# Multiplying decays out over 128 tokens in place of 64, with four working PSUM banks and an earlier VectorE step, in a fused gated-recurrence and ELU-layer kernel

## Chip, cores, metric

One core of one Trainium2 chip. The metric is device microseconds of one execution. Engine names: PE is TensorE, PEld its weight loads, DVE VectorE, ACT ScalarE, POOL GpSimd.

## The reference

```python
batch, n_heads, seq, head_dim = (4, 8, 768, 48)
for t in range(S):                       # complex state S, real output
    ar, ai = (a_re_n[:, :, t, :, None], a_im_n[:, :, t, :, None])
    new_re = ar * S_re - ai * S_im
    new_im = ar * S_im + ai * S_re
    kv = np.einsum('bhd,bhe->bhde', k[:, :, t], v[:, :, t])
    S_re, S_im = (new_re + kv, new_im)
    y[:, :, t] = np.einsum('bhd,bhde->bhe', q[:, :, t], S_re)
# then, on x = y as (3072, 384), with d_ff = 2048:
h = x @ w_in
g = np.where(h > 0.0, h, alpha * (np.exp(np.minimum(h, 0.0)) - 1.0))
return (g @ w_out).astype(np.float32)
```

The decay `a` is first cut to a magnitude of at most 0.999. The kernel works with its logarithm `l` (the magnitude) and its angle: sums over the tokens of a chunk, then exponentials and sines, turn the recurrence into matrix products inside a chunk plus a state carried between chunks.

## The kernel before

A unit is one tile of 128 tokens for two batches; there are 12 units (`u`). All matmuls are fp32. A program in slots interleaves the recurrence of one unit with the layer of earlier ones. Lines with "cut", and "..." within a call, mark what is left out.

```python
L = 64
def work(shape):                                   # working PSUM banks
    return ps.tile(shape, FP32, tag="w", bufs=3, name="w")
# ... cut ...
def ratios(u):                                     # GpSimd from the third unit on
    products(u).tensor_tensor(out=w, in0=x["ar"], in1=t, op=ALU.mult)
    products(u).tensor_tensor(out=t, in0=x["ai"], in1=t, op=ALU.mult)

def slopes(u):
    nc.vector.scalar_tensor_tensor(out=flat(t), in0=flat(w), ...)   # the angle's slope
    nc.vector.scalar_tensor_tensor(out=flat(lm), in0=flat(lm), ...) # l; needs no product of GpSimd
# ... cut ...
def scores(u, n):                                  # two 64-token blocks per head
    for h in range(H):
        for c in range(C // L):
            nc.tensor.matmul(t[ts(c, L), h], lhsT=x["kt", n][:, h, ts(c, L)],
                             rhs=x["qt", n][:, h, ts(c, L)], start=True, stop=True)
    nc.vector.tensor_tensor(out=x["a", n], in0=t, in1=mask..., op=ALU.mult)

def states(u, n):                                  # two states per tile
    for h in range(H):
        for c, g in enumerate(gs):
            nc.tensor.matmul(g[:, h], lhsT=x["kg"][ts(c, L), n, h],
                             rhs=vn[u % 2][ts(c, L), n, h, 0:D], start=True, stop=True)
    for c, g in enumerate(gs):                     # old None: first state, one product
        nc.vector.tensor_tensor(out=new_s, in0=g, in1=old, op=ALU.add)
        nc.gpsimd.tensor_tensor(out=new_s, in0=new_s, in1=wide, op=ALU.mult)

def values(u, n):                                  # output halves j, chunks c
    y = ps.tile([C, C // L, 512], FP32, tag="y", bufs=1, name="y")
    # a x v over 64 tokens for every (p, c, j), then state x q for every (p, c, j)
# ... cut ...
decays_of(u, r + 11, r + 12, r + 13.5, r + 14.5, r + 14.6, r + 15.5, r + 15.5, r + 15)
```

Of the kernel before, what the change touches and what calls it, by code (L numbers as in the profile page):

```python
# [10 lines left out]
FP32 = mybir.dt.float32  # L11
U32 = mybir.dt.uint32
AF = mybir.ActivationFunctionType
ALU = mybir.AluOpType
PSUM = bass.MemoryType.PSUM

C = 128
L = 64
CAP = 0.999
EPS = 1e-6  # L20
LEAST_RE = 0.7
# [46 lines left out]
HP = 64  # L68
# [436 lines left out]
def kernel(  # L505
# [12 lines left out]
    nc = tc.nc  # L518
    B, H, S, D = q.shape
    DM, DF = moe_w_in.shape[0], moe_w_out.shape[0]  # L520
    NI, NF = DM // C, DF // C
    NP = H // 2
    HD = H * D
    NB = 2
# [11 lines left out]
    ps = ctx.enter_context(tc.tile_pool(name="ps", bufs=1, space=PSUM))  # L536
    dram = ctx.enter_context(tc.tile_pool(name="dram", bufs=1, space=bass.MemoryType.DRAM))

    def const(a, name):
        a = np.ascontiguousarray(a, dtype=np.float32)  # L540
        t = cst.tile(list(a.shape), FP32, name=name)
        nc.sync.dma_start(out=t, in_=nc.inline_tensor(a, name=name + "_c").ap())
        return t
# [5 lines left out]

    i = np.arange(C)  # L550
    upto = i[:, None] <= i[None, :]
    own = i[:, None] // L == i[None, :] // L

    vn = [cst.tile([C, NB, H, HP], FP32, name=f"vn{n}") for n in range(2)]
    NR = 2 * NI * NF // (NI * WF)
# [3 lines left out]
    quarter = value(float(np.pi / 2), "quarter")  # L559

    def work(shape):
        return ps.tile(shape, FP32, tag="w", bufs=3, name="w")


    nat = [{} for _ in range(NU)]
# [97 lines left out]
    def flat(t):  # L663
        return t.rearrange("p n h d -> p (n h d)")
# [5 lines left out]
    def new(tag, bufs=1, shape=None):  # L670
        return sb.tile(shape or [C, NB, H, D], FP32, tag=tag, bufs=bufs, name=tag)
# [21 lines left out]
    def ratios(u):  # L693
# [2 lines left out]
        products(u).tensor_tensor(out=w, in0=x["ar"], in1=t, op=ALU.mult)  # L696
        products(u).tensor_tensor(out=t, in0=x["ai"], in1=t, op=ALU.mult)  # L697

    def slopes(u):
        x = nat[u]  # L700
        lm, e, w, t = x["m2"], x["e"], x["w"], x["t"]
        nc.vector.scalar_tensor_tensor(
            out=flat(t), in0=flat(w), scalar=-2.0, in1=flat(t), op0=ALU.add, op1=ALU.mult
        )
        nc.vector.scalar_tensor_tensor(  # L705
            out=flat(lm), in0=flat(lm), scalar=2 * float(np.log(CAP)), in1=flat(e),
            op0=ALU.min, op1=ALU.subtract,
        )
        x["l"] = lm

    def noted(u):

# [47 lines left out]
    def decays(u):  # L760
        x = nat[u]
        x["E"], x["F"] = new("n", 6), new("n", 6)
        x["T"] = new("T", 2, [2 * D, NB, C // L, H])
        for n in range(NB):
            t = work([C, HD])
            nc.tensor.matmul(  # L766
                t, lhsT=sum_logs, rhs=x["l"][:, n].rearrange("p h d -> p (h d)"),
                start=True, stop=True,
            )
            for key, sign in (("E", 1.0), ("F", -1.0)):  # L770
                nc.scalar.activation(  # L771
                    out=x[key][:, n].rearrange("p h d -> p (h d)"), in_=t, func=AF.Exp,
                    scale=sign,
                )
        ends = dram.tile([NB, C // L, H, D], FP32, tag="ends", bufs=2, name="ends")
        nc.scalar.dma_start(
            out=ends.rearrange("n c h d -> c n (h d)"),
            in_=x["E"][L - 1 :: L].rearrange("p n h d -> p n (h d)"),
        )
        x["ends"] = ends  # L780

# [9 lines left out]
    def gated(u):  # L791
        x = nat[u]
        shape = [C, NB * H, 2, D]
        for key, by in (("k", "F"), ("q", "E")):
            eng = products(u) if key == "k" else nc.vector
            g = x[key]
            eng.tensor_tensor(out=g, in0=g, in1=x[by], op=ALU.mult)
            o = new(key + "g", 1, shape)
            eng.tensor_tensor(  # L799
                out=o, in0=g.rearrange("p n h d -> p (n h) d").unsqueeze(2).to_broadcast(shape),  # L800
                in1=x["cs"], op=ALU.mult,
            )
            x[key + "g"] = o.rearrange("p (n h) i d -> p n h (i d)", n=NB)
        for i in range(2):
            nc.gpsimd.dma_start(
                out=x["T"][ts(i, D)].rearrange("p n c h -> p (n c h)"),
                in_=x["ends"].rearrange("n c h d -> d (n c h)"),
            )


# [10 lines left out]

    def scores(u, n):
        x = nat[u]
        t = work([C, H, L])
        for h in range(H):
            for c in range(C // L):
                nc.tensor.matmul(  # L827
                    t[ts(c, L), h], lhsT=x["kt", n][:, h, ts(c, L)],
                    rhs=x["qt", n][:, h, ts(c, L)], start=True, stop=True,
                )  # L830
        x["a", n] = new("a", 2, [C, H, L])
        nc.vector.tensor_tensor(  # L832
            out=x["a", n], in0=t, in1=mask.unsqueeze(1).to_broadcast([C, H, L]), op=ALU.mult
        )

    def states(u, n):

        x = nat[u]
        b, s = where(u)
        x["S", n] = [state.get(b + n)]  # L840
        if s == S - C:
            last = C // L - 1
        else:
            last = C // L
        gs = [work([2 * D, H, D]) for c in range(last)]
        for h in range(H):
            for c, g in enumerate(gs):
                nc.tensor.matmul(  # L848
                    g[:, h], lhsT=x["kg"][ts(c, L), n, h], rhs=vn[u % 2][ts(c, L), n, h, 0:D],
                    start=True, stop=True,  # L850
                )
        for c, g in enumerate(gs):
            old = x["S", n][-1]
            new_s = new("S", 9, [2 * D, H, D])
            wide = x["T"][:, n, c].unsqueeze(2).to_broadcast([2 * D, H, D])
            if old is None:
                nc.vector.tensor_tensor(out=new_s, in0=g, in1=wide, op=ALU.mult)
            else:
                nc.vector.tensor_tensor(out=new_s, in0=g, in1=old, op=ALU.add)  # L859
                nc.gpsimd.tensor_tensor(out=new_s, in0=new_s, in1=wide, op=ALU.mult)  # L860
            x["S", n].append(new_s)
        state[b + n] = x["S", n][-1]

    def values(u, n):
        x = nat[u]
        y = ps.tile([C, C // L, 512], FP32, tag="y", bufs=1, name="y")
        each = [(p, c, j) for p in range(NP) for c in range(C // L) for j in range(2)]
        for p, c, j in each:

            nc.tensor.matmul(  # L870
                y[ts(j, HP), c, ts(p, L)], lhsT=vn[u % 2][ts(c, L), n, 2 * p + j],
                rhs=x["a", n][ts(c, L), 2 * p + j], start=(p == 0), stop=False,
                skip_group_check=True,
            )
        for p, c, j in each:
            if x["S", n][c] is not None:
                nc.tensor.matmul(  # L877
                    y[ds(j * HP, D), c, ts(p, L)], lhsT=x["S", n][c][:, 2 * p + j],
                    rhs=x["qt", n][:, 2 * p + j, ts(c, L)], start=False, stop=False,
                    skip_group_check=True,  # L880
                )
        if n == 0:
            x["x"], x["y"] = new("x", 2, [C, NI, GT]), new("y", 1, [C, GT])

        nc.scalar.copy(  # L885
            out=x["x"][:, :, ts(n, C)].rearrange("p x (c t) -> p c x t", c=C // L),
            in_=y[:, :, 0 : NI * L].rearrange("p c (x t) -> p c x t", x=NI),
        )
        nc.scalar.copy(  # L889
            out=x["y"][:, ts(n, C)].rearrange("p (c t) -> p c t", c=C // L),  # L890
            in_=y[:, :, NI * L : NP * L],
        )

    def seam(u):
# [64 lines left out]
    load_a(0)  # L959
    ident = const(np.eye(C), "ident")  # L960
    sum_turns = const(upto / (2 * np.pi), "sum_turns")
    sum_logs = const((upto & own) * 0.5, "sum_logs")
    mask = const(upto[:, 0:L] | (i[:, None] >= L) & (i[:, None] - L <= i[None, 0:L]), "mask")
    for t in vn:
        nc.gpsimd.memset(t[:, :, :, D:HP], 0.0)
    ctx.enter_context(tc.manual_schedule())
# [29 lines left out]
        plan.append((at, len(plan), lambda: fn(*args)))  # L996

    def decays_of(u, *at):
        fns = squares, logarithms, ratios, slopes, noted, angles, carried, decays
        for x, fn in zip(at, fns):  # L1000
            put(x, fn, u)

# [23 lines left out]
    for at, fn, u in (  # L1026
        (-44, load_qk, 0), (-44, load_v, 0), (-42, load_a, 1), (-32.8, load_qk, 1), (-23.5, load_v, 1),
    ):
        put(at, fn, u)
    decays_of(0, -40, -39, -39, -38, -37.9, -38, -38, -35)  # L1030
    gates_of(0, -36.5, -36, -33)
    put(-34, warm, 30)
    values_of(0, -32, -31, -30, -29, -26, -28, -27, -25, -24, -23, -22)
    decays_of(1, -33.5, -32.5, -31.5, -30.8, -8, -30.7, -30.6, -26.5)
    gates_of(1, -27.5, -27, -22.5)
    values_of(1, -20, -19, -18, -17, -14, -16, -15, -13, -12, -11, -10)
    layer_of(0, 4, 20)
# [8 lines left out]
    for u in range(2, NU):  # L1046
        r = (u - 2) * SLOTS
        put(r, load_a, u)
        put(r + 1, load_v, u)
        put(r + 6, load_qk, u)  # L1050
        decays_of(u, r + 11, r + 12, r + 13.5, r + 14.5, r + 14.6, r + 15.5, r + 15.5, r + 15)
        gates_of(u, r + 17, r + 17.5, r + 19)
        values_of(u, *(r + 22 + x for x in (0, 1, 2, 3, 5, 4, 5, 6, 7, 8, 9)))
        layer_of(u, r + 36, r + 44)
# [42 lines left out]
```

## Time and profile before

| | before |
|---|---|
| median time | 790.8 us |
| TensorE busy, granted clock | 91%, 0.963 |
| period of a unit in the steady part | 58.70 us |
| TensorE's wait before the sum of logs | 19.2 us in 9 waits |

"Busy" adds up spans that overlap, so 91% is not time at the peak. The steady part is better read by its period, the distance between the starts of one unit's sum of logs and the next one's: whatever shortens the period is multiplied by the units.

```profile
493.85 0.96 DVE L702 SCALAR_TENSOR_TENSOR n<-n 128x768 f32<-128x768 f32 x1 [4.60 <-POOL n L697]
494.72 0.95 DVE L705 SCALAR_TENSOR_TENSOR n<-n 128x768 f32<-128x768 f32 x1
```

`l` (L705) stands behind the slope (L702), which needs GpSimd's two products (L696, L697), although `l` itself doesn't.

### The profile page before, as it was taken

What the parts mean: (1) busy time and instruction counts of PE and PEld (TensorE: products, weight loads), DVE (VectorE), ACT (ScalarE), POOL (GpSimd) and SP (SyncE); (2) the same over time, 40 slices, a digit from 0 to 9 for tenths busy, and PEclk for the clock granted to TensorE, in tenths of its full rate; (3) what the DMA queues carried; (4) which work ended last, traced back from release to release, by engine and by line L of the source; (5) the groups of instructions that cost most, each with busy time, mean ns of one, the idle gap of its engine ahead of it and who ended that gap; (6) DMA issues with size and microseconds to landing.
All of it is one profiled execution on the core that took longest, in us unless ns stands there. A gap on an engine that the chain in (4) does not pass through costs nothing.

```text
span 787.3 us, 12936 instructions
## 1 busy us (share of the span) xinstructions
PE 713.4 (91%) x5406; PEld 530.9 (67%) x5406; DVE 303.4 (39%) x394; ACT 388.4 (49%) x590; POOL 221.5 (28%) x206
## 2 busy tenths in 40 slices
PE   1566877999999999999999999999999999999996
PEld 0445766666587587587587587587587587686773
DVE  4659997521422531531531531531531531430110
ACT  6364237535456456456456456456456456552230
POOL 0023302122522523523523523523523513501000
PEclk9955799899999999999999999999999999999998
DMA  9997162320340540540540540530530630200000
GB/s 169 177 170 178 33 162 80 62 51 12 77 91 1 117 91 2 123 86 2 125 81 2 128 80 2 132 76 1 136 72 2 140 67 1 66 2 4 23 0 25
DMA packets 141452, 56.08 MB, mean 71 GB/s; under 512 B 128792, under 2 KB 133448, under 8 KB 140616
## 3 DMA queue, kind: packets, MB, share of 16 engines
q1 hardware_dynamic: 137536, 53.72, 31.6%
q0 software_dynamic: 3776, 1.36, 1.9%
q8 instruction: 44, 0.72, 0.4%
q14 instruction: 24, 0.20, 0.1%
q10 hardware_dynamic: 72, 0.07, 0.0%
HBM read 49.14 MB, written 4.79 MB: 68 GB/s over the span
## 4 chain that ended last, share of the span: by engine, by line
PE 75%; DVE 8%; POOL 5%; ACT 4%; issue 4%; DMA 2%; SPq 1%; POOLq 0%; DVEq 0%; ACTq 0%
PE mlp L911 29%; PE mlp L927 26%; PE w L819 6%; PE w L848 5%; PE w L827 3%; PE w L766 2%; POOL n L697 2%; POOL n L696 2%; PE w L744 2%; PE y L877 2%; DVE n L705 1%; DMA w<-in_moe_w_in_dram 1%; PE y L870 1%; POOL S L860 1%; DVE wf L42 1%
## 5 line engine op out<-in xcount | busy, mean ns | idle before, releaser
L911 PE MATMUL mlp<-x,w_in 128*128 128x256 f32 x1152 | 265.6, 386 | 4.0 <-DVE g L918 4.0
L927 PE MATMUL mlp<-w_out,g 128*128 128x384 f32 x768 | 261.9, 491 | 0.0
L911 PEld LDWEIGHTS mlp<-x,w_in 128*128 128x128 f32 x1152 | 218.9, 193 | 37.4 <-DVE g L918 4.4
L927 PEld LDWEIGHTS mlp<-w_out,g 128*128 128x128 f32 x768 | 142.2, 190 | 91.3
L918 DVE SCALAR_TENSOR_TENSOR g<-ee,mlp 128x512 f32<-128x512 f32 x96 | 66.0, 687 | 216.4 <-ACT ee L917 176.5
L916 ACT ACTIVATE ee<-mlp 128x512 f32<-128x512 f32 x96 | 57.2, 596 | 147.5 <-PE mlp L911 141.7
L860 POOL TENSOR_TENSOR S<-S,T 96x384 f32<-96x384 f32 x40 | 35.5, 888 | 251.4 <-DVE S L859 251.4
L917 ACT ACTIVATE ee<-ee 128x512 f32<-128x512 f32 x96 | 60.5, 630 | 2.8
L799 POOL TENSOR_TENSOR kg<-k,cs 128x1536 f32<-128x1536 f32 x10 | 48.1, 4814 | 16.8 <-issue 16.1
L680 POOL TENSOR_TENSOR n<-n 128x768 f32<-128x768 f32 x11 | 19.9, 1813 | 114.3 <-ACT n L678 114.3
L848 PEld LDWEIGHTS w<-vn,kg 64*96 64x96 f32 x704 | 37.3, 172 | 12.6 <-issue 9.0
L885 ACT COPY x<-y 128x384 f32<-128x384 f32 x24 | 11.5, 480 | 67.8 <-PE y L877 67.6
L848 PE MATMUL w<-vn,kg 64*96 64x48 f32 x704 | 40.5, 258 | 3.0 <-ACT n L771 3.0
L859 DVE TENSOR_TENSOR S<-w,S 96x384 f32<-96x384 f32 x40 | 22.1, 552 | 54.6 <-PE w L848 39.2
L933 ACT COPY o<-mlp 128x384 f32<-128x384 f32 x24 | 11.5, 480 | 61.7 <-PE mlp L927 59.7
L766 PE MATMUL w<-n,sum_logs 128*128 128x384 f32 x48 | 21.3, 568 | 20.7 <-DVE n L705 19.2
L832 DVE TENSOR_TENSOR a<-w,mask 128x512 f32<-128x512 f32 x24 | 16.5, 688 | 59.2 <-PE w L827 59.2
L820 ACT COPY qt<-w 96x512 f32<-96x512 f32 x48 | 25.5, 575 | 27.8 <-PE w L819 27.7
L899 POOL DMA_DIRECT2D x<-y x72 | 35.7, 503 | 4.5 <-ACT y L889 4.5
L758 POOL DMA_DIRECT2D carry<-n x10 | 5.1, 512 | 111.4 <-DVE n L752 93.0
L819 PE MATMUL w<-ident,qg 128*96 128x128 f32 x192 | 27.2, 286 | 9.7 <-DVE qg L799 9.0
L819 PE MATMUL w<-ident,kg 128*96 128x128 f32 x192 | 26.9, 284 | 9.7 <-ACT qt L820 9.6
(74 smaller groups left out, 756.0 us busy)
## 6 DMA issues: line engine op xcount, KB each, us to landing
w<-in_moe_w_out_dram SPq DMA_DIRECT2D x16, 768.0 KB
w<-in_moe_w_in_dram SPq DMA_DIRECT2D x8, 768.0 KB
ar<-in_a_re_dram SPq DMA_DIRECT2D x24, 192.0 KB
ai<-in_a_im_dram SPq DMA_DIRECT2D x24, 192.0 KB
w<-in_moe_w_in_dram SPq DMA_DIRECT2D x12, 384.0 KB
q<-in_q_dram SPq DMA_DIRECT2D x24, 192.0 KB
k<-in_k_dram SPq DMA_DIRECT2D x24, 192.0 KB
vn<-in_v_dram SPq DMA_DIRECT2D x24, 192.0 KB
```

The source lines that it names most:

```text
L766: nc.tensor.matmul(t, lhsT=sum_logs, rhs=x["l"][:, n].rearrange("p h d -> p (h d)"), start=True, stop=True,)
L799: eng.tensor_tensor(out=o, in0=g.rearrange("p n h d -> p (n h) d").unsqueeze(2).to_broadcast(shape), in1=x["cs"], op=ALU.mult,)
L819: nc.tensor.transpose(t[:, h], x[key + "g"][:, n, h0 + h], ident)
L820: nc.scalar.copy(out=o[:, h0 : h0 + 4], in_=t)
L848: nc.tensor.matmul(g[:, h], lhsT=x["kg"][ts(c, L), n, h], rhs=vn[u % 2][ts(c, L), n, h, 0:D], start=True, stop=True,)
L860: nc.gpsimd.tensor_tensor(out=new_s, in0=new_s, in1=wide, op=ALU.mult)
L899: nc.gpsimd.dma_start(out=x["x"][ds(j * HP + D, G), i], in_=x["y"][ds(j * HP + i * G, G)])
L911: nc.tensor.matmul(t[:, e], lhsT=w_in[:, i, ts(f + e, C)], rhs=x["x"][:, i], start=(i == 0), stop=(i == NI - 1),)
L916: nc.scalar.activation(out=e, in_=t, func=AF.Relu, scale=-1.0)
L917: nc.scalar.activation(out=e, in_=e, func=AF.Exp, scale=-1.0)
L918: nc.vector.scalar_tensor_tensor(out=x["g", f // 8][:, f % 8 : f % 8 + 2], in0=e, scalar=-1.0, in1=t, op0=ALU.add, op1=ALU.max)
L927: nc.tensor.matmul(x["o"], lhsT=x["g", f // 8][:, f % 8, ts(n, C)], rhs=w_out[:, f], start=(f == 0), stop=(f == NF - 1),)
```

## The change

It has three parts: decays run over the whole tile, so each head and tile has one score, one value and one state product; the working banks go from three to four (the value product needs one bank in place of two); and `l` gets a step of its own, `lengths`, ahead of `ratios`.

```diff
-        return ps.tile(shape, FP32, tag="w", bufs=3, name="w")
+        return ps.tile(shape, FP32, tag="w", bufs=4, name="w")
 # ... cut ...
+    def lengths(u):
+        x["l"] = lm = x["m2"]
+        nc.vector.scalar_tensor_tensor(out=flat(lm), in0=flat(lm), ...)
 # ... cut ... scores: two banks of four heads
-                    t[ts(c, L), h], lhsT=x["kt", n][:, h, ts(c, L)],
-                    rhs=x["qt", n][:, h, ts(c, L)], start=True, stop=True,
+                    t[:, h], lhsT=x["kt", n][:, h0 + h], rhs=x["qt", n][:, h0 + h],
+                    start=True, stop=True,
 # ... cut ... states: one per tile, none in a batch's last tile
-            last = C // L - 1
+            return
-                    g[:, h], lhsT=x["kg"][ts(c, L), n, h], rhs=vn[u % 2][ts(c, L), n, h, 0:D],
+                g[:, h], lhsT=x["kg"][:, n, h], rhs=vn[u % 2][:, n, h, 0:D], start=True,
 # ... cut ... values
-        y = ps.tile([C, C // L, 512], FP32, tag="y", bufs=1, name="y")
+        y = ps.tile([C, NP, C], FP32, tag="y", bufs=1, name="y")
 # ... cut ...
-        decays_of(u, r + 11, r + 12, r + 13.5, r + 14.5, ...)
+        decays_of(u, r + 11, r + 12, r + 13.4, r + 13.5, r + 14.5, ...)
```

More of the change, by code (lines that the diff above doesn't have):

```diff
@@ L17 @@
 C = 128
-L = 64
 CAP = 0.999
@@ L551 @@
     upto = i[:, None] <= i[None, :]
-    own = i[:, None] // L == i[None, :] // L
     vn = [cst.tile([C, NB, H, HP], FP32, name=f"vn{n}") for n in range(2)]
@@ L697, in ratios @@
         products(u).tensor_tensor(out=t, in0=x["ai"], in1=t, op=ALU.mult)
+    def lengths(u):
+        x = nat[u]
+        x["l"] = lm = x["m2"]
+        nc.vector.scalar_tensor_tensor(
+            out=flat(lm), in0=flat(lm), scalar=2 * float(np.log(CAP)), in1=flat(x["e"]),
+            op0=ALU.min, op1=ALU.subtract,
+        )
     def slopes(u):
         x = nat[u]
-        lm, e, w, t = x["m2"], x["e"], x["w"], x["t"]
+        w, t = x["w"], x["t"]
         nc.vector.scalar_tensor_tensor(
@@ L704, in slopes @@
         )
-        nc.vector.scalar_tensor_tensor(
-            out=flat(lm), in0=flat(lm), scalar=2 * float(np.log(CAP)), in1=flat(e),
-            op0=ALU.min, op1=ALU.subtract,
-        )
-        x["l"] = lm
     def noted(u):
@@ L762, in decays @@
         x["E"], x["F"] = new("n", 6), new("n", 6)
-        x["T"] = new("T", 2, [2 * D, NB, C // L, H])
+        x["T"] = new("T", 2, [2 * D, NB, H])
         for n in range(NB):
@@ L774, in decays @@
                 )
-        ends = dram.tile([NB, C // L, H, D], FP32, tag="ends", bufs=2, name="ends")
+        ends = dram.tile([NB, H, D], FP32, tag="ends", bufs=2, name="ends")
         nc.scalar.dma_start(
-            out=ends.rearrange("n c h d -> c n (h d)"),
-            in_=x["E"][L - 1 :: L].rearrange("p n h d -> p n (h d)"),
+            out=ends.rearrange("n h d -> (n h d)").unsqueeze(0), in_=flat(x["E"])[C - 1 : C]
         )
@@ L805, in gated @@
             nc.gpsimd.dma_start(
-                out=x["T"][ts(i, D)].rearrange("p n c h -> p (n c h)"),
-                in_=x["ends"].rearrange("n c h d -> d (n c h)"),
+                out=x["T"][ts(i, D)].rearrange("p n h -> p (n h)"),
+                in_=x["ends"].rearrange("n h d -> d (n h)"),
             )
@@ L823, in scores @@
         x = nat[u]
-        t = work([C, H, L])
-        for h in range(H):
-            for c in range(C // L):
+        x["a", n] = new("a", 1, [C, H, C])
+        for h0 in range(0, H, 4):
+            t = work([C, 4, C])
+            for h in range(4):
                 nc.tensor.matmul(
-                    t[ts(c, L), h], lhsT=x["kt", n][:, h, ts(c, L)],
-                    rhs=x["qt", n][:, h, ts(c, L)], start=True, stop=True,
-                )
-        x["a", n] = new("a", 2, [C, H, L])
-        nc.vector.tensor_tensor(
-            out=x["a", n], in0=t, in1=mask.unsqueeze(1).to_broadcast([C, H, L]), op=ALU.mult
-        )
+                    t[:, h], lhsT=x["kt", n][:, h0 + h], rhs=x["qt", n][:, h0 + h],
+                    start=True, stop=True,
+                )
+            nc.vector.tensor_tensor(
+                out=x["a", n][:, h0 : h0 + 4], in0=t,
+                in1=mask.unsqueeze(1).to_broadcast([C, 4, C]), op=ALU.mult,
+            )
     def states(u, n):
@@ L839, in states @@
         b, s = where(u)
-        x["S", n] = [state.get(b + n)]
+        x["S", n] = old = state.get(b + n)
         if s == S - C:
-            last = C // L - 1
-        else:
-            last = C // L
-        gs = [work([2 * D, H, D]) for c in range(last)]
-        for h in range(H):
-            for c, g in enumerate(gs):
-                nc.tensor.matmul(
-                    g[:, h], lhsT=x["kg"][ts(c, L), n, h], rhs=vn[u % 2][ts(c, L), n, h, 0:D],
-                    start=True, stop=True,
-                )
@@ L852, in states @@
-        for c, g in enumerate(gs):
-            old = x["S", n][-1]
-            new_s = new("S", 9, [2 * D, H, D])
-            wide = x["T"][:, n, c].unsqueeze(2).to_broadcast([2 * D, H, D])
-            if old is None:
-                nc.vector.tensor_tensor(out=new_s, in0=g, in1=wide, op=ALU.mult)
-            else:
-                nc.vector.tensor_tensor(out=new_s, in0=g, in1=old, op=ALU.add)
-                nc.gpsimd.tensor_tensor(out=new_s, in0=new_s, in1=wide, op=ALU.mult)
-            x["S", n].append(new_s)
@@ L862, in states @@
-        state[b + n] = x["S", n][-1]
+            return
+        g = work([2 * D, H, D])
+        for h in range(H):
+            nc.tensor.matmul(
+                g[:, h], lhsT=x["kg"][:, n, h], rhs=vn[u % 2][:, n, h, 0:D], start=True,
+                stop=True,
+            )
+        state[b + n] = new_s = new("S", 7, [2 * D, H, D])
+        wide = x["T"][:, n].unsqueeze(2).to_broadcast([2 * D, H, D])
+        if old is None:
+            nc.vector.tensor_tensor(out=new_s, in0=g, in1=wide, op=ALU.mult)
+        else:
+            nc.vector.tensor_tensor(out=new_s, in0=g, in1=old, op=ALU.add)
+            nc.gpsimd.tensor_tensor(out=new_s, in0=new_s, in1=wide, op=ALU.mult)
@@ L864, in values @@
     def values(u, n):
         x = nat[u]
-        y = ps.tile([C, C // L, 512], FP32, tag="y", bufs=1, name="y")
-        each = [(p, c, j) for p in range(NP) for c in range(C // L) for j in range(2)]
-        for p, c, j in each:
-            nc.tensor.matmul(
-                y[ts(j, HP), c, ts(p, L)], lhsT=vn[u % 2][ts(c, L), n, 2 * p + j],
-                rhs=x["a", n][ts(c, L), 2 * p + j], start=(p == 0), stop=False,
-                skip_group_check=True,
-            )
-        for p, c, j in each:
-            if x["S", n][c] is not None:
+        y = ps.tile([C, NP, C], FP32, tag="y", bufs=1, name="y")
@@ L877, in values @@
+        for p in range(NP):
+            for j in range(2):
                 nc.tensor.matmul(
-                    y[ds(j * HP, D), c, ts(p, L)], lhsT=x["S", n][c][:, 2 * p + j],
-                    rhs=x["qt", n][:, 2 * p + j, ts(c, L)], start=False, stop=False,
+                    y[ts(j, HP), p], lhsT=vn[u % 2][:, n, 2 * p + j],
+                    rhs=x["a", n][:, 2 * p + j], start=(p == 0), stop=False,
                     skip_group_check=True,
                 )
+        if x["S", n] is not None:
+            for p in range(NP):
+                for j in range(2):
+                    nc.tensor.matmul(
+                        y[ds(j * HP, D), p], lhsT=x["S", n][:, 2 * p + j],
+                        rhs=x["qt", n][:, 2 * p + j], start=False, stop=False,
+                        skip_group_check=True,
+                    )
@@ L885, in values @@
         nc.scalar.copy(
-            out=x["x"][:, :, ts(n, C)].rearrange("p x (c t) -> p c x t", c=C // L),
-            in_=y[:, :, 0 : NI * L].rearrange("p c (x t) -> p c x t", x=NI),
+            out=x["x"][:, :, ts(n, C)], in_=y[:, 0:NI],
         )
         nc.scalar.copy(
-            out=x["y"][:, ts(n, C)].rearrange("p (c t) -> p c t", c=C // L),
-            in_=y[:, :, NI * L : NP * L],
+            out=x["y"][:, ts(n, C)], in_=y[:, NI],
         )
@@ L961 @@
     sum_turns = const(upto / (2 * np.pi), "sum_turns")
-    sum_logs = const((upto & own) * 0.5, "sum_logs")
-    mask = const(upto[:, 0:L] | (i[:, None] >= L) & (i[:, None] - L <= i[None, 0:L]), "mask")
+    sum_logs = const(upto * 0.5, "sum_logs")
+    mask = const(upto, "mask")
     for t in vn:
@@ L998, in decays_of @@
     def decays_of(u, *at):
-        fns = squares, logarithms, ratios, slopes, noted, angles, carried, decays
+        fns = squares, logarithms, lengths, ratios, slopes, noted, angles, carried, decays
         for x, fn in zip(at, fns):
@@ L1029 @@
         put(at, fn, u)
-    decays_of(0, -40, -39, -39, -38, -37.9, -38, -38, -35)
+    decays_of(0, -40, -39, -37.95, -39, -38, -37.9, -38, -38, -35)
     gates_of(0, -36.5, -36, -33)
@@ L1033 @@
     values_of(0, -32, -31, -30, -29, -26, -28, -27, -25, -24, -23, -22)
-    decays_of(1, -33.5, -32.5, -31.5, -30.8, -8, -30.7, -30.6, -26.5)
+    decays_of(1, -33.5, -32.5, -30.75, -31.5, -30.8, -8, -30.7, -30.6, -26.5)
     gates_of(1, -27.5, -27, -22.5)
@@ L1050 @@
         put(r + 6, load_qk, u)
-        decays_of(u, r + 11, r + 12, r + 13.5, r + 14.5, r + 14.6, r + 15.5, r + 15.5, r + 15)
+        decays_of(u, r + 11, r + 12, r + 13.4, r + 13.5, r + 14.5, r + 14.6, r + 15.5, r + 15.5, r + 15)
         gates_of(u, r + 17, r + 17.5, r + 19)
```

## The prediction

> **What bounds the kernel now.** I read the page from the top: which engine is full, then in which stretch, then the chain that sets the end.
>
> ```profile
> span 787.3 us, 12936 instructions
> PE 713.4 (91%) x5406; PEld 530.9 (67%) x5406; DVE 303.4 (39%) x394; ACT 388.4 (49%) x590; POOL 221.5 (28%) x206
> PE   1566877999999999999999999999999999999996
> PEclk9955799899999999999999999999999999999998
> ```
>
> TensorE (PE) is full from about slice 8 (157 us) to the end at a granted clock near full; only the first fifth has holes. From there nothing but PE's own time, or a wait in PE's own row, can move the end. The chain of waits says the same (PE 75% of it), so I cut one period of the steady part out of it. A unit is two batches of 128 tokens with 8 heads; twelve units run, and from the third on each takes 58.7 us (the cumulative sum L766 starts at 378.42 and again at 437.12).
>
> ```profile
> 458.02 0.87 PE w L819 x8
> 458.90 2.59 PE mlp L911 x12
> 464.96 1.08 PE w L827 x32
> 466.04 2.79 PE mlp L911 x12
> 468.83 1.49 PE w L848 x32
> 470.32 2.79 PE mlp L911 x12
> 476.57 0.62 PE y L870 x32
> 477.20 1.03 PE y L877 x32
> 478.23 1.01 PE w L819 x8
> 479.24 2.58 PE mlp L927 x8
> 644.92 1.49 PE w L848 x16
> ```
>
> (start, length, what.) Scores (L827), states (L848) and values (L870, L877) stand as blocks between slices of the layer's matmuls (L911, L927), with no gap: they are paid in full. An fp32 matmul is two records, so 16 matmuls are x32; a transpose (L819) is one. A slice of the layer takes 2.59 us after a transpose but 2.79 after scores or states: 0.20 us is lost in coming back. So one batch now costs: scores 1.08 + 0.20 = 1.28; states 1.49 + 0.20 = 1.69; values 0.62 + 1.03 + 0.14 (the transpose behind them takes 1.01 in place of 0.87) or + 0.20 (where the layer follows), 1.82 on the mean. Sum 4.79 us.
>
> The last line is the most telling one. In the last two units only one 64-token half forms a state product: x16 records take the same 1.49 us as x32. The two halves run beside each other in the array, and the second is free.
>
> ```profile
> 437.12 1.53 PE L766 MATMUL w<-n,sum_logs 128*128 128x384 f32 x4 [1.44 <-DVE n L705]
> PE w L766 <- DVE n L705: 19.2, 9, 7.7
> 25.77 3.40 PE L989 MATMUL mlp<-ident 128*128 128x128 f32 x29
> ```
>
> The only steady hole in PE: once a unit the sum of the logs waits 1.44 us for VectorE's l. Nine such waits, one of 7.7 at the third unit, eight of 1.44. The third line is for pricing: full 128x128 fp32 matmuls of 128 columns at full clock, 3.40 us for 29 records, whose last outlasts its start by 0.28: 0.111 us a record.
>
> **What the Trainium skill says.** "TensorE: Matmul & The Clock Gate", section "LDWEIGHTS (loading the stationary operand)": the load takes the stationary columns over 1.2 GHz, whatever the rows. That is 80 ns for the 96 columns of the states, and the trace agrees: 1.49 us for 16 records is 93 ns each with entry and exit, more than 48 moving columns can need (a layer record streams 384 columns in 2.58/8 = 0.322 us, 0.84 ns a column, so 48 take 40 ns). "TensorEngine Tiling (Array Packing)", "Key Properties": changing the tiling mode drains TensorE, and different tiles load weights and multiply in parallel. The trace agrees with both: the 0.20 us above, and 32 score records of 64 columns (54 ns each) in 1.08 us. Against it, "Perfetto Trace Analysis", section "Matmuls", says larger matmuls are more efficient than smaller ones when possible; the x16 = x32 line shows where this need not hold, since the small ones here already share the array.
>
> **The change, part by part.** It halves the matmuls of every one of these blocks, and doubles rows, columns or both of each. What counts is array time.
>
> Scores: 8 matmuls with 128 stationary and 128 moving columns replace 16 of 64 by 64, two of which ran side by side. Half of the new product lies above the diagonal and is masked away, so the work has doubled. 16 records x 0.111 = 1.79 us; they are in the full-array mode like the layer, so I charge no drain. Before 1.28: +0.51.
>
> States: 8 matmuls over 128 rows replace 16 over 64. Rows are free, the 96-column load sets the pace: 16 records x 85 ns (80 and some 5) = 1.36, and 0.07 for the layer's first weight load that 40 ns of matmul can't cover: 1.43. Before 1.69: -0.26, from the drain alone.
>
> Values: 8 and 8 matmuls of 128 columns, alternating between the upper and lower output half. Before, L870 used four tiles at once (16 matmuls, 0.62), L877 two (1.03). Now both use two: 16 pairs of records x 128 columns x 0.84 ns = 1.72, plus the cost of entering and leaving a tiled mode, which I take from the scores of before (1.28 less 16 pairs x 54 ns = 0.42). 2.14 against 1.82: +0.32.
>
> Sum 5.36 against 4.79, +0.57 us a batch, and 20 batches in the full part: +11.4 us. Fewer instructions, more time.
>
> Skipped states: the last token tile of each batch needs no state any more (before: one half). Four blocks of 1.43 that I have just counted go: -5.7.
>
> The wait: l now is formed on VectorE ahead of GpSimd's two products (1.81 us each) in place of behind them. Its inputs come from ScalarE some 7 us before PE wants it. -8 x 1.44 = -11.5. At the third unit VectorE is behind with converting weights, and l moves up only past a g, the end of one conversion and the start of the next: from 139.7 to about 137, -2.5.
>
> Does the wait return one step later, at the sum of turns (L744), which needs the angles that still go through GpSimd? PE reached it at 443.64, its last input was there at 443.30. That is only 0.3 us of slack; but the angles' ScalarE work stands behind the exponentials of L766, so it moves up with L766, and GpSimd's products start earlier too (one state update of 0.89 us where there were two). I expect no new wait.
>
> Off the path: VectorE masks twice as much (24 more of 0.688, +16.5) and adds 24 fewer states of 0.552 (-13.2), in 303 of 787 us; GpSimd loses 24 of 0.888; PSUM stays at 8 banks (4+1+3 for 3+2+3). These cost or earn nothing. Before 157 us, where PE has holes, VectorE gains four masks and loses four adds, and score blocks at half clock are longer: +0.5.
>
> Total: 11.4 - 5.7 - 11.5 - 2.5 + 0.5 = -7.8; 790.8 - 7.8 = **783 us**.
>
> **Rivals.** (1) Halving the instructions halves the blocks: 20 x 4.79 / 2 = 48 us, to about 725. For it: the records and the row total of PE busy, which adds overlapping spans (L848 40.5 us, L827 29.2). Against it: x16 = x32 in 1.49 us. (2) The two output halves don't share the array at 128 columns with 128 rows: values take 1.7 us more a batch, +35, to 818. Against it, the state part of the values with 96 rows, 1.03 us for 32 records; nothing in the trace shows it for 128 columns. (3) The wait moves to L744 in full: only the array terms stay, 783 + 11.5 = 795. The slack of 0.3 speaks for it, the order on ScalarE against it. (4) The early part turns: VectorE is the bound there up to about 106 us, and any microsecond on its chain shifts all; 3 us either way. (5) Scores also drain (96 rows, not 128): +0.35 x 20 = 7, to 790.
>
> **Range and chances.** My total is a small difference of larger terms (+11.4, -5.7, -14.0), each good to about 3 us, with the early part good to 3: 775 to 792. Faster by over 2% (below 775) needs nearly all array terms to be cheaper than priced: 10%. Slower by over 2% (above 806.6) needs rival 2: 5%. Within 2%: 85%.
>
> **What will show it.** In the chain of the changed kernel: scores x16 at 1.7 to 1.9 us, states x16 at about 1.4, the two value blocks x16 at about 0.9 each, no wait before the sum of logs, a period of about 58.7 - 1.44 + 1.14 = 58.4 us. A period of 55 or less shows rival 1; value blocks at 1.7, rival 2; a wait on L744, rival 3. If the period is as said and the total isn't, the early part is where to look.

## More of the kernel before

Why the sum of logs waits is seen in two timelines of the kernel before, of GpSimd and of VectorE (start, length, instruction, and in brackets the idle time ahead of it and what ended it):

```profile
489.33 0.83 POOL L860 TENSOR_TENSOR S<-S,T 96x384 f32<-96x384 f32 x1 [0.67 <-DVE S L859]
490.11 1.81 POOL L696 TENSOR_TENSOR n<-ar,n 128x768 f32<-128x768 f32 x1
492.00 1.81 POOL L697 TENSOR_TENSOR n<-ai,n 128x768 f32<-128x768 f32 x1
```

GpSimd's two products (L696, L697) stand behind the second state update of the tile (L860).

## The result

| | before | changed |
|---|---|---|
| median time | 790.85 us | 773.52 us |
| ratio (95% interval) | | 0.9763 (0.973 to 0.9796) |
| period of a unit | 58.70 us | 57.93 us |
| third unit's sum of logs starts at | 139.68 us | 134.42 us |
| from there to the end of the span | 647.7 us | 637.4 us |

Ratios here and below are the mean time of one kernel's runs over that of the other's in the same rounds, so they are not quite the ratio of the medians quoted. The time lies below the predicted range of 775 to 792. All outputs are right.

Two lines of the changed kernel's page, and one of its waits:

```profile
span 771.8 us, 9827 instructions
PE 712.5 (92%) x3870; PEld 548.3 (71%) x3870; DVE 305.1 (40%) x394; ACT 388.0 (50%) x590; POOL 199.5 (26%) x182
```
```profile
PE w L767 <- DVE n L700: 4.8, 1, 4.8
```

Of the 3,109 instructions that are gone, 1,536 are TensorE's multiplications and 1,536 its weight loads (5406 - 3870 each), and yet TensorE's busy sum has moved by only 0.9 us. Of the nine waits before the sum of logs one is left. The chain of waits of the changed kernel, over one unit's first batch and the values of it:

```profile
455.27 1.79 PE w L828 x16
457.05 2.59 PE mlp L904 x12
459.65 1.32 PE w L846 x16
460.96 2.66 PE mlp L904 x12
467.09 1.02 PE y L864 x16
468.11 0.88 PE y L872 x16
468.99 1.01 PE w L819 x8
```

Read against the prediction's lines of before: scores (L828) take 1.79 us and the layer behind them is back at its full-array 2.59, so they cost 1.79 where 1.08 + 0.20 stood. States (L846) take 1.32 with 0.07 behind them. Values (L864, L872) take 1.02 + 0.88 + 0.14, or + 0.20 where the layer follows. A batch costs 1.79 + 1.39 + 2.07 = 5.25 us, against 4.79: half the matmuls, and more array time.

So the time did not come from the products in the steady part. 10.3 us came after the third unit's sum of logs (647.7 - 637.4), where 5.8 was predicted, and the rest, 5.3 us in these profiles and some 7 by the medians (17.3 - 10.3), from before it, where 2.0 was predicted.

### The profile page after: what moved, and what is told of

Read it like the earlier page. It is cut to its first block, busy times and chain, and to the rows that moved or that the text cites. A ratio compares the mean times of both kernels' runs of the same rounds, so it can differ in the third digit from the quotient of the medians.

```text
span 771.8 us, 9827 instructions
## 1 busy us (share of the span) xinstructions
PE 712.5 (92%) x3870; PEld 548.3 (71%) x3870; DVE 305.1 (40%) x394; ACT 388.0 (50%) x590; POOL 199.5 (26%) x182
## 3 DMA queue, kind: packets, MB, share of 16 engines
q0 software_dynamic: 3392, 1.29, 1.1%
## 4 chain that ended last, share of the span: by engine, by line
PE 84%; DVE 7%; ACT 4%; DMA 2%; issue 2%; SPq 1%; DVEq 0%; ACTq 0%
PE mlp L920 31%; PE mlp L904 30%; PE w L828 5%; PE w L819 5%; PE w L846 3%; PE y L864 3%; PE y L872 2%; PE w L767 2%; PE w L745 2%; DVE wf L41 1%; DMA w<-in_moe_w_in_dram 1%; DVE wp L48 1%; DVE wp L44 1%; DVE wf L38 1%; DMA ai<-in_a_im_dram 1%
## 5 line engine op out<-in xcount | busy, mean ns | idle before, releaser
L904 PE MATMUL mlp<-x,w_in 128*128 128x256 f32 x1152 | 262.9, 384 | 5.1 <-DVE g L911 5.1
L856 POOL TENSOR_TENSOR S<-S,T 96x384 f32<-96x384 f32 x16 | 18.4, 1149 | 165.6 <-DVE S L855 165.6
L828 PEld LDWEIGHTS w<-qt,kt 96*128 96x128 f32 x384 | 48.8, 200 | 12.5 <-ACT kt L820 9.0
L832 DVE TENSOR_TENSOR a<-w,mask 128x512 f32<-128x512 f32 x48 | 32.0, 687 | 64.1 <-PE w L828 64.1
L828 PE MATMUL w<-qt,kt 96*128 96x128 f32 x384 | 49.7, 285 | 8.1 <-ACT kt L820 8.1
L880 ACT COPY x<-y 128x384 f32<-128x384 f32 x24 | 11.5, 478 | 68.1 <-PE y L872 60.2
L926 ACT COPY o<-mlp 128x384 f32<-128x384 f32 x24 | 11.5, 480 | 61.7 <-PE mlp L920 59.7
L745 PE MATMUL w<-n,sum_turns 128*128 128x384 f32 x48 | 20.2, 550 | 16.6 <-ACT n L728 16.6
L846 PEld LDWEIGHTS w<-vn,kg 128*96 128x96 f32 x320 | 31.4, 171 | 5.3 <-ACT n L772 2.1
L819 PEld LDWEIGHTS w<-ident,qg 128*96 128x96 f32 x192 | 23.4, 136 | 16.4 <-DVE qg L799 13.8
```

The source lines that it names most:

```text
L745: nc.tensor.matmul(t, lhsT=sum_turns, rhs=x["th"][:, n].rearrange("p h d -> p (h d)"), start=True, stop=True,)
L819: nc.tensor.transpose(t[:, h], x[key + "g"][:, n, h0 + h], ident)
L828: nc.tensor.matmul(t[:, h], lhsT=x["kt", n][:, h0 + h], rhs=x["qt", n][:, h0 + h], start=True, stop=True,)
L832: nc.vector.tensor_tensor(out=x["a", n][:, h0 : h0 + 4], in0=t, in1=mask.unsqueeze(1).to_broadcast([C, 4, C]), op=ALU.mult,)
L846: nc.tensor.matmul(g[:, h], lhsT=x["kg"][:, n, h], rhs=vn[u % 2][:, n, h, 0:D], start=True, stop=True,)
L904: nc.tensor.matmul(t[:, e], lhsT=w_in[:, i, ts(f + e, C)], rhs=x["x"][:, i], start=(i == 0), stop=(i == NI - 1),)
```

## The experiments

### The place of l alone

The kernel before, with `l` moved and nothing else:

```diff
-        fns = squares, logarithms, ratios, slopes, noted, angles, carried, decays
+        fns = squares, logarithms, lengths, ratios, slopes, noted, angles, carried, decays
-        decays_of(u, r + 11, r + 12, r + 13.5, r + 14.5, ...)
+        decays_of(u, r + 11, r + 12, r + 13.4, r + 13.5, r + 14.5, ...)
```

> The kernel before with nothing changed but the place of l: on VectorE ahead of GpSimd's products. If TensorE is the only bound and the wait before the sum of logs is worth its 1.44 us plus about 0.24 us of restart (the sum of logs takes 1.53 us after the wait and 1.29 us in the changed kernel, which has none), the period falls from 58.70 to 57.02 us and the profiled span to about 787.3 - 8 x 1.68 - 3 = 771 us, as good as the whole change: the products over 128 tokens would then be worth nothing in sum. If the wait is worth 1.44 alone: 57.26 us and 773. If it moves to the sum of turns: about 58.5 us and 785.

Measured: median 773.59 us, ratio 0.978 (0.9756 to 0.9804), span 770.2 us, the period 57.03 us. From the chain of waits of this kernel:

```profile
482.41 1.29 PE w L769 x4
483.70 5.16 PE mlp L930 x16
```

The sum of logs takes 1.29 us here, where it took 1.53 behind its wait. A wait costs its length and then a restart: 58.70 - 57.03 = 1.67 us a unit, not the 1.44 that the waits' row shows. This one moved instruction does as much as the whole change, and the wait didn't move on to the sum of turns.

### The products and banks alone

The changed kernel, with `l` put back behind GpSimd's products (the reverse of the edit above).

> The changed kernel with l put back behind GpSimd's products. If what held l up was the second state update in GpSimd's queue, one state product per tile removes the steady wait as well, and the period stays at 57.9 to 58.1 us; only the wait at the third unit comes back (4.8 to some 7.7 us): about 775 us. If the place of l is what removes the wait, it comes back in full: a period of 57.93 + 1.68 = 59.6 us, about 788 to 790 us.

Measured: 777.83 us, ratio 0.9827 (0.9803 to 0.9851), the period 57.99 us. The chain of waits at the end of a unit:

```profile
487.05 2.78 PE mlp L917 x8
489.83 1.35 PE w L764 x4
```

GpSimd's timeline ahead of it:

```profile
483.17 0.82 POOL L853 TENSOR_TENSOR S<-S,T 96x384 f32<-96x384 f32 x1 [4.91 <-DVE S L852]
483.95 1.80 POOL L694 TENSOR_TENSOR n<-ar,n 128x768 f32<-128x768 f32 x1
```

The steady wait is gone here too, to 0.06 us (1.35 for 1.29): with one state update a tile GpSimd starts its products early enough, and VectorE has `l` ready at 489.50, just before the sum of logs starts at 489.66. (The fourth bank is in this kernel too. No run took it away while `l` stood behind; with `l` in front it leaves the period as it is, see below.) So the two parts are substitutes. Each takes away the same wait by itself, and together they can't take it away twice. Only the third unit's wait needs the early `l`: 7.7 us here, 4.8 in the changed kernel and in the one with `l` alone in front.

### The order of the output halves

```diff
-        for p in range(NP):
-            for j in range(2):
+        for j in range(2):
+            for p in range(NP):
```

in both value loops of the changed kernel.

> The changed kernel with the value products in another order: all of the upper output half, then all of the lower. Theory: two of them share the array only because they alternate between the halves. Then a record stands alone with 128 columns x 0.84 ns = 0.107 us, 16 records take 1.75 us in place of 0.88 to 1.02, 44 blocks lose 0.86 us each, and the time is about 773.5 + 38 = 811 us. Rival, that the order is of no account: 773.5 us.

Measured: 784.65 us, ratio 0.991 (0.9882 to 0.9937), the period 59.07 us. Both theories miss: 1.14 us more a unit, 0.57 a block, where 0.86 or nothing was expected. The timeline of TensorE suggests why the loss is smaller:

```profile
429.89 1.25 PE L864 MATMUL y<-a,vn 128*64 128x128 f32 x13
430.88 0.31 PE L872 MATMUL y<-qt,S 96*48 96x128 f32 x1
430.98 0.27 PE L864 MATMUL y<-a,vn 128*64 128x128 f32 x1
431.02 0.27 PE L872 MATMUL y<-qt,S 96*48 96x128 f32 x1
431.09 0.27 PE L864 MATMUL y<-a,vn 128*64 128x128 f32 x1
```

All of L864 stands ahead of all of L872 in the program, yet the first L872 starts ahead of three L864. I read this so: each output half goes through its own work, and one can be ahead of the other, so the two still overlap in part. Alternating them is 0.57 us a block cheaper, but without it the sharing isn't lost altogether.

### One change of tiling mode less

This experiment uses a mixed kernel (mixed_ends, told of below), whose units 3 to 9 are the same as with `l` alone in front. Its values of a unit's first batch are moved to stand directly ahead of the scores of the second.

```diff
-        values_of(u, *(r + 22 + x for x in (0, 1, 2, 3, 5, 4, 5, 6, 7, 8, 9)))
+        values_of(u, *(r + 22 + x for x in (0, 1, 2, 3, 6, 4, 5, 6, 7, 8, 9)))
```

> As mixed_ends, with the values of a unit's first batch moved down to stand directly ahead of the scores of its second, with no full-array work between them. Theory: what these blocks cost beyond their streaming is entry to and exit from a tiled mode of the array, so one exit and entry less a unit saves about 0.3 us: period 56.7 in place of 57.03 us in units 3 to 9, 3 us in all or less. Rival, that the 0.2 us belongs to each block whatever its neighbours: 57.03.

Measured: period 56.74 us in place of 57.03, as expected; 766.85 us, ratio 0.9685 (0.9653 to 0.9717). In its chain of waits values (L927, L934) and scores (L845) stand together:

```profile
467.45 0.62 PE y L927 x32
468.08 1.03 PE y L934 x32
469.11 0.93 PE w L845 x32
```

The scores take 0.93 here where they took 1.08 after the layer. So a part of what these small blocks cost beyond their streaming belongs to the change between them and the full-array work, 0.29 us for one exit and entry, and it can be saved by the order alone. This fits the drain at a change of tiling mode that the Trainium skill ("TensorEngine Tiling (Array Packing)", "Key Properties") names.

### Four banks or three

```diff
-        return ps.tile(shape, FP32, tag="w", bufs=4, name="w")
+        return ps.tile(shape, FP32, tag="w", bufs=3, name="w")
```

in the changed kernel, twice.

> The changed kernel with three working banks in place of four. Theory: TensorE's blocks stand apart by slices of the layer, so no block waits for a bank in the steady part: period 57.9 us, time within 0.3% of the changed kernel's 773.5 us. Rival, that the fourth bank is part of the gain: a wait for a copy appears before scores or transposes, 0.3 us or more a unit, and 3 us or more in all.

> The changed kernel with three working banks again, with more rounds. The earlier runs agree from the third unit on to 0.3 us, but the first profile was 2.1 us later by then. Theory: the fourth bank lets the early transposes run ahead of ScalarE's copies; from the copy of the first k to the first k product of the second unit it is 21.6 us in the four profiles with four banks of plain order and 22.5 with three. So 1 to 2.5 us more than the changed kernel. Rival, that this is the scatter of TensorE's clock in the early part: the medians agree within 0.7 us.

Measured: 775.48 us, ratio 0.9785 (0.975 to 0.982), unclear against the changed kernel's 0.9763; then, in five rounds, 777.75 us, 0.9824 (0.9806 to 0.9842), against 0.9774 (0.9754 to 0.9795) for the changed kernel. The second pair of intervals doesn't overlap. The differences of the ratios are 0.0022 and 0.005, or 1.7 and 4 us of 791. The period is 57.93 us in both: all of it is in the early part.

Profiles of the early part can't be compared by clock time alone, because the second unit's `ai` (the imaginary part of its decays) lands at a different time in each execution. ScalarE's first instruction on it starts between 36.98 and 41.60 us in the 14 profiles, and TensorE's first scores start 8.19 to 8.25 us after that in all of them, with three banks or four. Counted from that instruction, the layer's first matmul comes after 50.5 to 51.9 us in the five profiles of the 128-token kernel with four banks and no added work, and after 52.6 to 54.3 us in the six with three banks and 128-token products in the first two units.

So the expected cause, the early transposes, isn't the one: with three banks half of the first k's transposes do wait for a copy, but the first scores start no later. The banks part at the first unit's second batch. First three banks (the second of these runs), then four, in the timelines of TensorE and VectorE:

```profile
63.22 1.16 PE L828 MATMUL w<-qt,kt 96*128 96x128 f32 x8
67.22 2.08 PE L828 MATMUL w<-qt,kt 96*128 96x128 f32 x8 [2.84 <-ACT n L772]
69.33 0.69 DVE L832 TENSOR_TENSOR a<-w,mask 128x512 f32<-128x512 f32 x1 [2.02 <-PE w L828]
```
```profile
60.66 2.05 PE L828 MATMUL w<-qt,kt 96*128 96x128 f32 x16
63.57 1.28 DVE L832 TENSOR_TENSOR a<-w,mask 128x512 f32<-128x512 f32 x2
```

With three banks the second half of these scores waits for ScalarE's exponentials of the next unit's sum of logs, which hold the bank, and VectorE then waits 2.02 us for the scores. (In the first of these runs it is 0.90, with TensorE at a higher clock just then: 1.16 us for the same x8.) With four the scores go through at once and VectorE doesn't wait. All six profiles with three banks and 128-token products have this wait of VectorE's, and none of the six with four. The prediction counted the banks and said that they earn nothing. That holds in the steady part, and fails where TensorE is latency-bound.

### The dropped state work put back in the first two units

```diff
             nc.vector.tensor_tensor(out=new_s, in0=g, in1=wide, op=ALU.mult)
+            extra = new("S", 7, [2 * D, H, D])
+            nc.vector.tensor_tensor(out=extra, in0=g, in1=new_s, op=ALU.add)
+            nc.gpsimd.tensor_tensor(out=extra, in0=extra, in1=wide, op=ALU.mult)
```

in the changed kernel; it runs four times, in the branch without an older state.

> The changed kernel, with the state add on VectorE and the state product on GpSimd that it dropped in the first two units put back four times as work on a spare tile. Theory: VectorE sets the early part, each add stands in its row (0.55 to 0.65 us), and GpSimd's product beside it slows VectorE's next instruction (the k product took 2.27 us in the kernel before against 1.75 in the changed one), so the first matmul of the layer comes some 2 to 3 us later and the time grows by 1.5 to 3 us. Rival, that VectorE waits there anyway: no change.

Measured: 778.25 us, ratio 0.9823 (0.9803 to 0.9843) against 0.9774 for the changed kernel: some 4 us by the ratios and 6 by the medians, more than expected, for four adds of 0.55. VectorE's timeline, first with the work put back, then in the changed kernel (its lengths are to be compared, not its starts: `ai` landed 2.75 us later in the first):

```profile
70.44 0.94 DVE L797 TENSOR_TENSOR k<-k,n 128x768 f32<-128x768 f32 x1
71.42 2.27 DVE L799 TENSOR_TENSOR kg<-k,cs 128x1536 f32<-128x1536 f32 x1
```
```profile
67.10 0.94 DVE L797 TENSOR_TENSOR k<-k,n 128x768 f32<-128x768 f32 x1
68.08 1.76 DVE L799 TENSOR_TENSOR kg<-k,cs 128x1536 f32<-128x1536 f32 x1
```

The k product takes 2.27 us beside GpSimd's state product and 1.76 without it. The Trainium skill ("Perfetto Trace Analysis", "Optimizing Scalar/DVE Operations") says that the two engines share an SBUF read port; the trace agrees, with 0.51 us for one such meeting. Two more meetings stand in the same timeline: L631 at 86.55 us takes 1.74 in place of 1.23, and L38 at 95.74 takes 1.07 in place of 0.56. The first of the four adds meets nothing and falls where VectorE is idle. So a dropped state saves VectorE its add and, where GpSimd's product would have met a VectorE instruction, about half a microsecond more. Three adds and three meetings of about 0.5 us are some 3 of the 4 us; the rest isn't traced.

### 64 tokens in the middle, 128 at the ends

The kernel with `l` in front, with the changed kernel's products for some units only (`whole_of`): 0 and 1 (called mixed_first in the expectations), or 0, 1, 10 and 11 (mixed_ends). Both sets of constants are kept, and there are three working banks, since the 64-token values need two banks of their own. To fit, `a` has one buffer and `y` shares the buffer of `rnd`.

```diff
+    whole_of = lambda u: u in (0, 1, 10, 11)
-                t, lhsT=sum_logs, rhs=x["l"][:, n].rearrange("p h d -> p (h d)"),
+                t, lhsT=sum_all if whole_of(u) else sum_logs, rhs=x["l"][:, n].rearrange("p h d -> p (h d)"),
 # ... cut ... scores, states and values branch on whole_of(u)
```

> The changed kernel unaltered, on the same chip and in the same rounds as the next three, so that they can be compared with it: 773.5 us, period 57.93 us.

> The kernel before with l in front (773.6 us), but the first two units multiply their decays out over 128 tokens as the change does; units 2 to 11 stay at 64. Theory: the early part is set by VectorE, which loses four state adds there and the waits for them, while its extra masks lie mostly where it waits for TensorE anyway. From the totals so far the change gains about 3.6 us there (the changed kernel and the one with l alone in front end within 0.1 us of each other although the first takes 3.6 us more from the third unit's sum of logs on). So 770 to 771.5 us, with the first matmul of the layer 1.5 to 3 us earlier than 91.7. Rival, that the difference lies in the clock of single runs: 773.6.

> As mixed_first, and the last two units over 128 tokens as well: they need no state then. From the traces, the stretch from the last sum of logs but one to the end takes 170.5 us in the changed kernel and 173.9 with l alone in front: another 3.4 us. Theory: 766.5 to 768 us, 0.7 to 0.9% below the changed kernel. Rival, that the skipped states are given back by the larger scores and values (0.76 us a batch by the block lengths, 3.0 in four): under 1 us gained.

Measured: the changed kernel 772.41 us, ratio 0.9757 (0.9734 to 0.978); first units only 775.7 us, 0.9785 (0.9751 to 0.9819); both ends 770.79 us, 0.9739 (0.9715 to 0.9763). The first is a miss: nothing gained over `l` alone in front (0.978), and the layer's first matmul came at 94.6 us in place of the expected 88.7 to 90.2. Part of that lateness is `ai`, which landed 3.3 us later in this profile than with `l` alone in front. Counted from there the layer's first matmul comes after 54.3 us (52.6 to 53.0 in the three later mixed kernels), against 54.7 with `l` alone in front and 50.5 to 51.9 in the changed kernel. So with three banks the products over 128 tokens earn 0.4 to 2.1 us there in the profiles, and nothing that the times show, which fits the bank experiment. In the last units the skipped states pay: the two ratios differ by 0.0046, 3.6 us of 791, near the 3.4 expected. Their intervals overlap a little, but the profiles agree: from the third unit's sum of logs to the end it is 634.3 and 630.3 us.

To see whether the late start in these profiles is due to loading both sets of constants first, the 64-token set was loaded later, in the kernel with fewer mode changes:

```diff
-    sum_logs = const((upto & own) * 0.5, "sum_logs")
+    put(-1.5, late_constants)          # sum_logs and mask of the 64-token units
```

> The changed kernel once more, for comparison with the next three in the same rounds: 772 to 774 us; first matmul of the layer at 89.7 to 90, third unit's sum of logs at about 134.5.

> As mixed_ends_fewer_modes (766.9 us), with the two constants of the 64-token units loaded after the start in place of in front of the first weights and q, k. In the kernels with both sets loaded first the first copy of k ended at 49.3 to 50.5 us in place of 46 to 48. If that is the loads' doing, 2 to 3 us come back: 764 us. If it is scatter: 766.9.

Measured: changed kernel 771.95 us; late constants 766.39 us, ratio 0.969 (0.9667 to 0.9713), no different from 0.9685: the times show no gain from the edit. The copy of the first k ended anywhere from 45.7 to 50.5 us in the profiles. It follows the landing of the second unit's `ai`, which scatters as much (above). What moves that landing isn't shown.

The last kernel and the one with fewer mode changes beat both kernels. Their ratios are 0.969 and 0.9685, where the changed kernel had 0.9774 and 0.9757, and they use 64-token products in the units 2 to 9.

## Why the prediction was wrong

**Right.** That TensorE's row sets the steady part and that half the matmuls would cost more array time, not less: 5.25 us a batch against a predicted 5.36 and 4.79 before. Scores were 1.79 as predicted, states 1.39 for 1.43, values 2.07 for 2.14. With `l` in front in both, the 128-token products are 57.93 - 57.03 = 0.90 us a unit slower than the 64-token ones. Rival 1, that the blocks halve, is dead; so is rival 2 (values 1.02 and 0.88 us), 3 (no wait at the sum of turns) and 5 (no drain behind the scores). The skipped states, with the larger scores and values of the same two units, came to 173.9 - 170.5 = 3.4 us in the traces, against 5.7 - 4 x 0.57 = 3.4.

**Wrong in size: "The wait".** The term was -8 x 1.44 = -11.5. With `l` alone in front, the stretch from the third unit's sum of logs to the end fell from 647.7 to 633.8 us (770.2 less its start at 136.42): 13.9. Most of the missing 2.4 is the restart after a wait, 8 x (1.53 - 1.29) = 1.9 us. With the batches at +3.6 net of the skipped states (637.4 - 633.8) in place of +5.7, this is the whole of the 4.5 us that the steady part was off. The third unit's wait (-2.5) measured 7.74 - 4.80 = -2.9.

**Wrong in kind: the two terms "These cost or earn nothing" and "+0.5" for the early part.** This is the larger failure, and rival 4 named only its size ("3 us either way"), not its cause. Apart from the third unit's wait the early part gained 5.3 - 2.9 = 2.4 us in the profiles and about 4 by the medians, where a loss of 0.5 was predicted. I had balanced four masks against four adds on VectorE. The runs show two things in place of that. The fourth bank spares VectorE a wait for the scores of the first unit's second batch (1.7 to 4 us by the times). A dropped state is worth its add and the meeting with GpSimd's product on VectorE, about 4 us for four. Against these stand the doubled masks and the longer scores at half clock. By difference they cost some 2 to 5 us; no run measured them alone, and the landing of `ai` alone scatters by 4.6 us over the profiles, so that division stays rough. Counted from that landing, the layer's first matmul came after 54.5 us in the kernel before and after 50.5 to 51.9 in three profiles of the changed one.

**What the chain of reasons missed as a whole.** The diff has three parts, and I priced the early `l` and the products as if each had its own effect. They overlap on the steady wait. That the steady sum was off by no more than 4.5 us is partly luck: I credited the wait to the early `l` alone and never asked whether the dropped state update would remove it by itself.

## What to carry to other kernels

Count array time and not matmuls: small matmuls that share the array in tiles may be cheaper than the large one that replaces them, and their real overhead is the change of mode, which the order of blocks can save. When a diff has several parts, ask of each wait which of them would remove it alone. And price the latency-bound start by itself: there a bank or a short VectorE instruction is paid in full which is free in the steady part. Before two profiles of such a start are compared, count both from the input that landed last.

## What the Trainium skill lacked or had wrong

- "TensorE: Matmul & The Clock Gate", "The mechanism" (Part 3): it says that matmuls start and end in program order. In the run with one half at a time a record of L872 started at 430.88 us, ahead of one of L864 at 430.98 that precedes it in the program and writes the other output half. The starts contradict the page; the ends in a trace are modelled and decide nothing.
- "Perfetto Trace Analysis", "Matmuls": that larger matmuls are more efficient needs a limit. With `l` in front in both, the period is 57.03 us with 64-token products that share the array, and 57.93 with 128-token ones.
- "TensorEngine Tiling (Array Packing)", "Key Properties": it names the drain at a mode change without a price. Here the layer's slice took 0.20 us longer on return from scores, and one exit and entry less saved 0.29 us a unit (57.03 to 56.74).
- "TensorE: Matmul & The Clock Gate", "Back-to-back issue gap": its formula doesn't say that it isn't for fp32; the passes of fp32 stand elsewhere in the skill, so a pointer is missing and not the fact. Here an fp32 matmul of 256 columns is two records of 216 ns each (2.59 us for 12).
- No page prices a restart of a stream of fp32 matmuls after a wait (the nearest is the latency of a single bf16 matmul): 1.53 us in place of 1.29 for the same four records, and 1.67 us a unit for a wait of 1.44.
- "Perfetto Trace Analysis", "Optimizing Scalar/DVE Operations": the shared port of VectorE and GpSimd has no price there, though other pages say more of it. Here three VectorE instructions took 0.51 us longer each (1.76 to 2.27, 1.23 to 1.74, 0.56 to 1.07), and GpSimd's state product took 1.47 us beside a VectorE instruction where it took 0.83 alone.
